# Two layers of attention and feed-forward in a planned kernel: when integer-route scores are sent, when GELU may begin, and GpSimd's effect in the planner's model

## The chip, the cores and the metric

The kernel runs on one core of one Trainium2 chip. The metric is the device time of one execution in microseconds (us). The kernel before took 1625.61 us, the median of three runs (1623.0 to 1626.69).

## What is computed

A sequence of 2048 tokens with 512 features passes through attention, feed-forward, attention and feed-forward again, each on a layer norm of its input and each added to the input. Both attentions share their weights, and so do both feed-forwards. There are 32 heads of 16 features, and the feed-forward is 1376 wide.

```python
def _A_ref(x, wqkv, wo):
    B, S, D = x.shape
    H = 32; Dh = D // H
    qkv = (lambda x, *d: x.transpose(*d))((x @ wqkv).reshape(B, S, 3, H, Dh), 2, 0, 3, 1, 4)
    q, k, v = qkv[0], qkv[1], qkv[2]
    scale = Dh ** -0.5
    scores = jnp.einsum("bhqd,bhkd->bhqk", q, k) * scale
    p = _softmax(scores, axis=-1)
    o = jnp.einsum("bhqk,bhkd->bhqd", p, v)
    return (lambda x, *d: x.transpose(*d))(o, 0, 2, 1, 3).reshape(B, S, D) @ wo
def _B_ref(x, w1, b1, w2, b2):
    y = _layernorm(x, axis=-1)
    h = _gelu(jnp.einsum("bsd,df->bsf", y, w1) + b1)
    return jnp.einsum("bsf,fd->bsd", h, w2) + b2
x = A_x
x = x + _A_ref(_layernorm(x, axis=-1), A_wqkv, A_wo)
x = x + _B_ref(_layernorm(x, axis=-1), B_w1, B_b1, B_w2, B_b2)
x = x + _A_ref(_layernorm(x, axis=-1), A_wqkv, A_wo)
x = x + _B_ref(_layernorm(x, axis=-1), B_w1, B_b1, B_w2, B_b2)
```

## The kernel before

**A planner writes the program.** Before anything is compiled, a small simulation in Python decides the order of the instructions on every engine. A job is a generator (`job_ffn`, `flow_scores` and others). It yields a `Task` for one engine, with a priority (smaller is more urgent) and a list of instructions, each with what it reads and writes and a duration in us; or it yields a condition: `keys` (events that must have been marked), `get` (a buffer from a pool), `ready` (the planner's clock has come near the time at which some data will be there). `Sched.run` (L437) picks again and again the task that could start earliest, by `best` (L380), where among those that are ready the priority decides. `Prog.op` (L105) then appends the instructions to their engine's stream and moves that engine's clock on by the modelled duration. So a modelled duration, a priority or a condition costs nothing on the chip by itself; it only decides the order. On the chip each engine runs its stream in that order, with semaphore waits between engines. A second pass, `refill` (L1176), puts matmuls on zeros (`zw`, L1281 to L1285) into gaps of TensorE (PE)[...].

**Scores.** `L` is 1 for the first pair of layers and 3 for the second. A *segment* (`build_segments`, L515) is one group of four heads (`hg`, 8 of them) with one unit of 512 queries (`qc`), against the keys of a part of the sequence. Mostly a segment has 64 *tiles*, each of 128 keys by 512 queries for one head. The first unit of each layer is cut in two parts by keys, of 16 and 48 tiles in the first layer and 48 and 16 in the second, and the last unit of the second layer is cut into two halves of 256 queries, whose segments have 32 tiles. That makes 88 segments with 4096 tiles. `flow_scores` (L1293) sends groups of three and two tiles in turn to PE (L1372, banks 0 to 4 of PSUM, four row tiles of 32 at once); each group goes through one exponential on ScalarE (ACT, L1357) into a buffer `PT`.

**The integer route.** Of every 16 blocks of 128 keys, five (`DK`) may be done without ScalarE. VectorE (DVE) takes the score tile from PSUM, adds a constant and writes 16-bit integers, whose bits read as bf16 are a coarse exponential (`d_load`, L1449). Three copies follow with the integer shifted by 32, 64 and 96 (`job_d`, L1480, two tiles at a time), and four PV matmuls with differently weighted values (`vs`) stand where one stood, so that the errors cancel. `take_d` (L1382) decides whether such a tile may be sent. It refuses when more than one score is on its way (`dload`), when VectorE's planned end is over 1.3 us ahead or over 2.0 us of its tasks are pending, when four batches are in work, when neither of its two PSUM banks (5, `DLANE`, and 7, `MISCB`, which projections and feed-forward use too) is near to being free, and, with fewer than 8 tiles left in the segment, when the next segment has already had four (two in the beginning). `take_d` is asked when a group is sent (`flow_scores`), when the planner sees a gap of over 0.5 us on PE (`fill_pe`), and by `d_solo` (L1429), which runs at the end of each load and first asks that VectorE's planned end and all its pending tasks add up to 1.2 us at most (`D_IDLE`).

**PV.** `try_pv` (L1497) sends the second matmuls (L1546, four column tiles at once, priority 1.0) into one accumulator, bank 6. At the end of a segment `job_segend` empties it by a transpose on VectorE (L1576); only then may the next segment's PV begin.

**Feed-forward.** When the eight segments of a unit are done, `job_post` runs the projection (L1632), residual (L1656) and norm (L832 to L845), and `job_ffn` (L1695) the first matmuls (L1687) with bias adds on VectorE (L1711), GELU on ScalarE as two instructions (L1717, ten blocks, and L1718, the last one), priority -1.0, which need another table than the exponential, the second matmuls (L1725), and residuals (L1727). In the first layer the norm and QKV of the second follow (`job_lnqkv`: L902, L908, L915, L925, scale L1088, queries L1118); in the second, the stores of the output (L1740). A unit's first matmuls wait until the unit before it is through. The priority of this work on PE is 2.2, and 0.95 for the last two units of the first layer. The last unit has its own end (`job_tail`).

**GpSimd (POOL)** makes the weighted values (L1143), the merges of the cut units (L1604 to L1607) and small things of the norms. `ln_apply` (L845), the query scaling (L1118) and the shifts (L1480) are VectorE instructions between tensors in SBUF. In the model of before, GpSimd does not affect them.

Of the kernel before, what the change touches and what calls it, by code (L numbers as in the profile page):

```python
# [14 lines left out]
ALU = mybir.AluOpType  # L15
# [48 lines left out]
class Prog:  # L64


    def __init__(self):
# [10 lines left out]
        self.drain = 0.0  # L78
        self.work = []
# [25 lines left out]
    def op(self, eng, fn, reads=(), writes=(), same_ok=(), dur=0.3, lat=None):  # L105
# [3 lines left out]
        q = None  # L109
        if eng == "sp":  # L110
            q = self.dma_rr
            self.dma_rr = (self.dma_rr + 1) % NDMAQ
            writes = writes + (("dmaq", q),)
        op = _Op(eng, fn, reads, writes)
# [23 lines left out]
        else:  # L138
            op.t1 = op.t0 + dur
# [131 lines left out]
class Sched:  # L271
# [4 lines left out]
    def __init__(self):  # L276
# [9 lines left out]
        self.filler = None  # L286

# [149 lines left out]
    def run(self):  # L437
        while True:
# [12 lines left out]
            t = pick[1]  # L451
# [8 lines left out]
            if t.cb is not None:  # L460
                t.cb()
        if self.live or self.kwait:
# [15 lines left out]
D_GAP = 0.5  # L478
DLANE = 5
D_IDLE = 1.2  # L480
D_PRIO = 0.5
# [16 lines left out]
class Builder:  # L498
# [344 lines left out]
    def ln_apply(self, tt, slot, i, dst, dres, prio):  # L843
        c = 4 * slot + i
        return Task("dve", prio, [I(lambda e: e.tensor_scalar(out=dst, in0=self.xres[:, tt, :], scalar1=self.mv[:, c, 0:1], scalar2=self.rs[:, c:c + 1], op0=ALU.subtract, op1=ALU.mult),  # L845
                                    [("x", tt), ("mv", c), ("rs", slot)], [dres], 0.407)])
# [263 lines left out]
    def job_qt(self, sg, s):  # L1110
# [8 lines left out]
                                  [RS, ("scl", k), ("qbias",)], [("qt", q)], 0.18 + 0.24 * W / 512)])  # L1119
# [8 lines left out]
    def job_vs(self, sg, i, kbs):  # L1128
# [9 lines left out]
        if L == 1:  # L1138
# [5 lines left out]
                                   [("V", hg, kb) for kb in kbs], [("vs", q, i + k2) for k2 in range(n)], 0.209 + 0.17 * n, [("vs", q, i + k2) for k2 in range(n)] if k > 1 else []) for k in (1, 2, 3)])  # L1144
# [148 lines left out]
    def flow_scores(self):  # L1293
# [11 lines left out]
        while True:  # L1305
# [14 lines left out]
            while len(grp) < G:  # L1320
# [4 lines left out]
                grp.append((sg, (sg["todo"] or sg["todod"]).pop(0)))  # L1325
            banks = list(range(b0, b0 + len(grp)))
# [102 lines left out]
    def d_solo(self):  # L1429

        S_ = self.S_
        if not self.wide or self.P.free["dve"] - S_.now + sum(o[4] for t in S_.pend["dve"] for o in t.ops) > D_IDLE:
            return
# [38 lines left out]
    def job_d(self, bt):  # L1472
# [4 lines left out]
        for k in range(1, len(SHIFT)):  # L1477
# [3 lines left out]
                                     [("dp", u, w) for w in range(n)], [("dp", v, w) for w in range(n)] + self.dres(v), 0.150 + 0.2605e-3 * N)])  # L1481
# [87 lines left out]
    def job_segend(self, sg):  # L1569
# [28 lines left out]
        if nparts == 2:  # L1598
# [5 lines left out]
            yield Task("pool", 1.2, [I(lambda e: e.tensor_tensor(out=M, in0=M, in1=dw.unsqueeze(2).broadcast_to([128, 16, 16]), op=ALU.mult), [RW, RO], [RO], 0.62),  # L1604
                                     I(lambda e: e.tensor_tensor(out=den, in0=den, in1=dw, op=ALU.mult), [RW, RD], [RD], 0.25),
                                     I(lambda e: e.tensor_tensor(out=T[:, :, 16], in0=T[:, :, 16], in1=den, op=ALU.add), [RD, RA], [RA], 0.26),
                                     I(lambda e: e.tensor_tensor(out=T[:, :, 0:16], in0=T[:, :, 0:16], in1=M, op=ALU.add), [RO, RA], [RA], 0.75)])  # L1607
# [87 lines left out]
    def job_ffn(self, L, qc):  # L1695
# [20 lines left out]
        HR = [("h", k) for k in range((NFC + 1) // 2)]  # L1716
        yield Task("act", -1.0, [I(lambda e: e.activation(out=self.gv[:, 0:nf * W], in_=hv[:, 0:nf * W], func=ACTF.Gelu_apprx_tanh), HR, HR, 1.5 + 0.427 * nf * W / 512, (), 1.313 + 0.2 + 0.427 * nf * W / 512),  # L1717
# [99 lines left out]
    def build(self):  # L1817
# [27 lines left out]
        S_.filler = self.fill_pe  # L1845
# [61 lines left out]
```

## Time and profile before

| | |
|---|---|
| median of three runs | 1625.61 us |
| the profiled execution | 1622.21 us, its span 1620.4 us |
| busy time: ACT, DVE, POOL | 1539.1 us, 1463.8 us, 195.9 us |
| exponentials (L1357) | 1288 for 3188 tiles, 1463.6 us |
| loads of the integer route (L1449) | 908, mean 680 ns |
| its shifts (L1480) | 1383, mean 422 ns |
| long GELUs (L1717) begin, after their table load | 332.8, 510.8, 694.9, 892.2, 1121.1, 1303.0, 1493.7 us; a short one 1587.4 us |
| a table load | 1283 ns |

Times in lines of the profile are us from the start of the span unless marked ns. PE is TensorE's matmuls, PEld its weight loads; L with a number is a line of the kernel's source. In a line of a group, the last part is the idle time of the engine just ahead of these instructions and what ended most of it; in a line of waits, the numbers are us in total, times and the longest. In a timeline, neighbouring records of one line are merged (x3), and brackets hold the idle time before the first.

### The profile page before, as it was taken

What the parts mean: (1) busy time and instruction counts of PE and PEld (TensorE: products, weight loads), DVE (VectorE), ACT (ScalarE), POOL (GpSimd) and SP (SyncE); (2) the same over time, 40 slices, a digit from 0 to 9 for tenths busy, and PEclk for the clock granted to TensorE, in tenths of its full rate; (3) what the DMA queues carried; (4) which work ended last, traced back from release to release, by engine and by line L of the source; (5) the groups of instructions that cost most, each with busy time, mean ns of one, the idle gap of its engine ahead of it and who ended that gap; (6) DMA issues with size and microseconds to landing.
All of it is one profiled execution on the core that took longest, in us unless ns stands there. A gap on an engine that the chain in (4) does not pass through costs nothing.

```text
span 1620.4 us, 39194 instructions
## 1 busy us (share of the span) xinstructions
PE 1582.4 (98%) x16531; PEld 481.8 (30%) x16531; DVE 1463.8 (90%) x3283; ACT 1539.1 (95%) x1369; POOL 195.9 (12%) x406
## 2 busy tenths in 40 slices
PE   9999999999999999999999999999999999999998
PEld 3222222222222222222222322222222222344454
DVE  7899999988998889979999799999899989999792
ACT  6998999999999999989999999999999999999993
POOL 4354210000100001001111124200000000000000
PEclk9999999999999999999999999999999999999999
DMA  6662011212311321224523232211102000121100
GB/s 173 118 159 66 21 30 25 60 30 69 90 47 33 65 70 44 63 60 107 104 44 63 62 92 40 56 29 24 27 16 46 21 25 15 40 47 33 39 22 21
DMA packets 212465, 88.80 MB, mean 55 GB/s; under 512 B 183835, under 2 KB 206656, under 8 KB 212288
## 3 DMA queue, kind: packets, MB, share of 16 engines
q1 hardware_dynamic: 212288, 86.29, 23.1%
q8 instruction: 129, 2.11, 0.6%
q14 instruction: 48, 0.39, 0.1%
HBM read 34.65 MB, written 19.48 MB: 33 GB/s over the span
## 4 chain that ended last, share of the span: by engine, by line
PE 43%; ACT 31%; DVE 22%; issue 2%; POOL 1%; DMA 0%; POOLq 0%; DVEq 0%
ACT PT L1357 29%; PE ps L1372 14%; PE ps L1546 12%; DVE dp L1449 8%; DVE dp L1480 6%; PE ps L1725 4%; PE ps L1687 4%; PE ps L902 3%; PE ps L1281 2%; ACT h L1717 2%; DVE accT L1576 1%; PE ps L1632 1%; DVE st L832 1%; DVE xn L1585 1%; PE ps L1283 1%
## 5 line engine op out<-in xcount | busy, mean ns | idle before, releaser
L1357 ACT ACTIVATE PT<-ps 128x1024 bf16<-128x1024 f32 (+1 forms) x1288 | 1463.6, 1273 | 44.9 <-PE ps L1372 39.9
L1372 PE MATMUL ps<-QT,KT 32*128 32x512 bf16 (+1 forms) x4608 | 680.6, 359 | 16.0 <-DVE dp L1449 7.6
L1449 DVE TENSOR_SCALAR dp<-ps 128x512 uint16<-128x512 f32 x908 | 608.5, 680 | 66.5 <-PE ps L1372 62.3
L1480 DVE TENSOR_SCALAR dp<-dp 128x1024 uint16<-128x1024 uint16 (+1 forms) x1383 | 525.0, 422 | 8.5 <-PE ps L1546 4.0
L1546 PE MATMUL ps<-PT,V 128*17 128x512 bf16 (+1 forms) x3583 | 469.4, 358 | 1.1 <-DVE accT L1576 1.1
L1546 PE MATMUL ps<-dp,vs 128*17 128x512 bf16 (+1 forms) x3075 | 435.5, 357 | 0.4 <-DVE dp L1480 0.2
L1372 PEld LDWEIGHTS ps<-QT,KT 32*128 32x128 bf16 x4608 | 169.0, 91 | 542.7 <-ACT PT L1357 271.6
L1283 PE MATMUL ps<-zw 32*128 32x444 bf16 (+2 forms) x814 | 223.8, 324 | 0.0
L1546 PE MATMUL ps<-dp,V 128*17 128x512 bf16 (+1 forms) x1025 | 205.1, 358 | 2.9 <-DVE accT L1576 2.7
L1285 PE MATMUL ps<-zw 128*32 128x448 bf16 (+17 forms) x1552 | 149.4, 324 | 0.6 <-DVE accT L1576 0.6
L1546 PEld LDWEIGHTS ps<-dp,vs 128*17 128x17 bf16 x3075 | 110.7, 88 | 127.8 <-issue 102.8
L1546 PEld LDWEIGHTS ps<-PT,V 128*17 128x17 bf16 x3583 | 111.1, 88 | 111.5 <-issue 99.1
L1281 PE MATMUL ps<-zw 128*128 128x448 bf16 (+22 forms) x573 | 137.1, 335 | 4.0 <-DVE ps L711 1.7
L840 POOL TENSOR_SCALAR rs<-mv 128x4 f32<-128x4 f32 (+2 forms) x19 | 4.3, 225 | 906.6 <-DVE mv L833 905.1
L1687 PE MATMUL ps<-yT,wf 128*128 128x512 bf16 (+3 forms) x396 | 103.0, 360 | 0.9 <-DVE yT L1808 0.5
L902 PE MATMUL ps<-wqkv,xnT 128*128 128x512 bf16 x336 | 92.8, 384 | 1.4 <-DVE qk L915 0.8
L1143 POOL TENSOR_SCALAR vs<-V 128x340 bf16<-128x340 bf16 (+2 forms) x72 | 61.1, 849 | 141.8 <-PE ps L1546 138.2
L1281 PEld LDWEIGHTS ps<-zw 128*128 128x128 bf16 x573 | 44.2, 98 | 88.8 <-issue 54.4
L1711 DVE TENSOR_SCALAR h<-ps,b1c 128x512 bf16<-128x512 f32 (+2 forms) x88 | 61.8, 702 | 7.1 <-PE ps L1687 6.9
L1546 PEld LDWEIGHTS ps<-dp,V 128*17 128x17 bf16 x1025 | 48.5, 88 | 53.4 <-issue 30.1
L1283 PEld LDWEIGHTS ps<-zw 32*128 32x128 bf16 x814 | 61.2, 92 | 1.6
L1576 DVE STREAM_TRANSPOSE accT<-ps 128x512 f32<-128x512 f32 (+1 forms) x88 | 57.9, 658 | 3.4 <-PE ps L1546 2.8
(171 smaller groups left out, 886.9 us busy)
## 6 DMA issues: line engine op xcount, KB each, us to landing
vs<-vs_scr SPq DMA_DIRECT2D x56, 255.0 KB, 2.6
wf<-in_B_w_dram SPq DMA_DIRECT2D x90, 128.0 KB, 2.6
q_scr<-qk SPq DMA_DIRECT2D x22, 256.0 KB, 2.1
k_scr<-qk SPq DMA_DIRECT2D x12, 256.0 KB, 2.0
out_dram<-xres SPq DMA_DIRECT2D x16, 128.0 KB, 1.7
vs_scr<-vs SPq DMA_DIRECT2D x8, 255.0 KB, 3.1
xres<-in_A_x_dram SPq DMA_DIRECT2D x7, 256.0 KB, 3.7
v_scr<-vst SPq DMA_DIRECT2D x12, 136.0 KB, 1.8
```

The lines of the kernel that those rows point to most:

```text
L902: yield Task("pe", prio, [I(lambda e, c=c: e.matmul(self.ps[:, b, :], lhsT=xnT[:, c, :], rhs=self.wqkv[:, c, which * 512:which * 512 + 512 ...
L1281: fn = lambda e: e.matmul(self.ps[:, b, 0:w], lhsT=self.zw[:, 0:128], rhs=self.zw[:, 0:w], start=st, stop=st, skip_group_check=True)
L1283: fn = lambda e: e.matmul(self.ps[:, b, 0:w], lhsT=self.zw[32 * p:32 * p + 32, 0:128], rhs=self.zw[32 * p:32 * p + 32, 0:w], start=st, sto ...
L1285: fn = lambda e: e.matmul(self.ps[32 * p:32 * p + 32, b, 0:w], lhsT=self.zw[:, 0:32], rhs=self.zw[:, 0:w], start=st, stop=st, skip_group_c ...
L1357: S_.submit(Task("act", 1e-5 * gi, [I(lambda e, pt=pt, n=n, b0=b0: e.activation(out=self.PT[:, pt:pt + n, :], in_=self.ps[:, b0:b0 + n, :] ...
L1372: return [I(lambda e, kb=kb, i=i: e.matmul(self.ps[:, b, i * W:(i + 1) * W], lhsT=self.KT[32 * hp:32 * hp + 32, hg, kb * 128:(kb + 1) * 12 ...
L1449: self.S_.submit(Task("dve", 0.0, [I(lambda e: e.tensor_scalar(out=self.dp[:, u, w * 512:(w + 1) * 512], in0=self.ps[:, b, :], scalar1=BIT ...
L1480: yield Task("dve", pr, [I(lambda e, k=k, v=v: e.tensor_scalar(out=self.dp[:, v, 0:N], in0=self.dp[:, u, 0:N], scalar1=float(SHIFT[k]), sc ...
L1546: ops.append((nth[j, sh] + 0.1 * i, I(lambda e, hp=hp, v=v, ap=ap[:, i * W:(i + 1) * W], first=first and i == 0, W=W: e.matmul(self.ps[32 ...
L1576: yield Task("dve", 0.3, [I(lambda e: e.transpose(self.accT[:, a, 0:W], self.ps[:, ACCB, 0:W]), [("ps", ACCB)], [RA], 0.17 + 0.535 * W / 5 ...
L1687: yield Task("pe", pr, [I(lambda e, c=c: e.matmul(self.ps[0:M, b, off:off + W], lhsT=self.w1(fc, c), rhs=self.yT[:, c, 0:W], start=(c == 0 ...
L1725: yield Task("pe", pr, [I(lambda e, fc=fc, i=i, b=b: e.matmul(self.ps[:, b, :], lhsT=self.gt(fc, i, W), rhs=self.w2(L, fc), start=(fc == 0 ...
```

## The change

It has three parts, all in the planner; no instruction is added to or taken from the program but for what follows from how many tiles take which route.

First, `d_solo` is asked after every VectorE task that has been planned (`after_dve`), besides at the end of each load, and it counts as pending only those tasks that can start within 0.5 us (`D_NEAR`). The conditions in `take_d` stay.

Second, before GELU is handed to ScalarE, `job_ffn` waits until its input is nearly there, and then for a mark of the scores: of the current segment 30% of the tiles must have been taken, and where more than 50% have been already, it is the next segment whose 30% is waited for. In the last segment there is no such wait.

Third, the model knows of GpSimd: `Prog.op` keeps the last GpSimd instruction's start, end and effect (`hit`), and a VectorE instruction marked "fast" that overlaps it is planned longer by 0.09 (L1143), 0.28 (L1604) or 0.38 us (L1607). Two base durations are set a little lower.

```diff
--- before.py
+++ after.py
@@ -76,6 +76,7 @@
         self.tiling = "full"
         self.tiles = {}
         self.drain = 0.0
+        self.hit = (0.0, 0.0, 0.0)
         self.work = []
 
     def ready(self, eng, reads, writes, same_ok=()):
@@ -136,6 +137,13 @@
             self.work.append((op.t0, op.t1, 1.0 if how == "full" else 0.25))
             self.free[eng] = op.t0 + min(dur, PE_ISSUE)
         else:
+            if eng == "pool":
+                self.hit = (op.t0, op.t0 + dur, lat or 0.0)
+                lat = None
+            elif lat == "fast":
+                if self.hit[0] < op.t0 + dur and op.t0 < self.hit[1]:
+                    dur += self.hit[2]
+                lat = None
             op.t1 = op.t0 + dur
             self.free[eng] = op.t0 + (max(0.02, dur - OVERLAP[eng]) if lat is None else lat)
         deps = {}
@@ -284,6 +292,7 @@
         self.live = 0
         self.timers = []
         self.filler = None
+        self.after_dve = None
 
     def submit(self, task, cb=None):
         self.seq += 1
@@ -459,6 +468,8 @@
                 self.P.op(t.eng, fn, reads, writes, same_ok, dur, lat)
             if t.cb is not None:
                 t.cb()
+            if t.eng == "dve" and self.after_dve is not None:
+                self.after_dve()
         if self.live or self.kwait:
             raise RuntimeError("scheduler stuck: %d live, keys %s, pools %s" % (self.live, list(self.kwait)[:8], [(n, len(p.free), len(p.waiters)) for n, p in self.pools.items() if p.waiters]))
 
@@ -476,8 +487,11 @@
 FILL_SLACK = 0.02
 READ_SLACK = 0.4
 D_GAP = 0.5
+GELU_FROM = 0.3
+GELU_TO = 0.5
 DLANE = 5
 D_IDLE = 1.2
+D_NEAR = 0.5
 D_PRIO = 0.5
 DBATCH = 2
 DFLY = 4
@@ -843,7 +857,7 @@
     def ln_apply(self, tt, slot, i, dst, dres, prio):
         c = 4 * slot + i
         return Task("dve", prio, [I(lambda e: e.tensor_scalar(out=dst, in0=self.xres[:, tt, :], scalar1=self.mv[:, c, 0:1], scalar2=self.rs[:, c:c + 1], op0=ALU.subtract, op1=ALU.mult),
-                                    [("x", tt), ("mv", c), ("rs", slot)], [dres], 0.407)])
+                                    [("x", tt), ("mv", c), ("rs", slot)], [dres], 0.395, (), "fast")])
 
     def dma(self, fn, reads, writes, prio, dur=0.08, lat=None):
         return Task("sp", prio, [I(fn, reads, writes, dur, (), lat)])
@@ -1116,7 +1130,7 @@
         W = sg["W"]
         src, RS = (self.psbf(self.q0bank)[:, 0:512], ("ps", self.q0bank)) if s is None else (self.qraw[:, s, 0:W], ("qraw", s))
         yield Task("dve", 0.4, [I(lambda e: e.tensor_scalar(out=self.QT[:, q, 0:W], in0=src, scalar1=self.scl[:, k, hg:hg + 1], scalar2=self.qbias[:, 0:1], op0=ALU.mult, op1=ALU.add),
-                                  [RS, ("scl", k), ("qbias",)], [("qt", q)], 0.18 + 0.24 * W / 512)])
+                                  [RS, ("scl", k), ("qbias",)], [("qt", q)], 0.16 + 0.24 * W / 512, (), "fast")])
         if s is None:
             self.S_.release("mb", self.q0bank)
         else:
@@ -1141,7 +1155,7 @@
         yield ("keys", self.kv_keys(sg, kbs))
         src = self.V[:, hg, kbs[0]:kbs[-1] + 1:3, :, :].rearrange("p k h d -> p k (h d)")
         yield Task("pool", 0.8, [I(lambda e, k=k: e.tensor_scalar(out=self.vs[:, q, k - 1, i:i + n, :], in0=src, scalar1=WSHIFT[k], scalar2=None, op0=ALU.mult),
-                                   [("V", hg, kb) for kb in kbs], [("vs", q, i + k2) for k2 in range(n)], 0.209 + 0.17 * n, [("vs", q, i + k2) for k2 in range(n)] if k > 1 else []) for k in (1, 2, 3)])
+                                   [("V", hg, kb) for kb in kbs], [("vs", q, i + k2) for k2 in range(n)], 0.209 + 0.17 * n, [("vs", q, i + k2) for k2 in range(n)] if k > 1 else [], 0.09) for k in (1, 2, 3)])
         for kb in kbs:
             self.S_.mark(("vs", sg["i"], kb))
         d = DK.index(kbs[0])
@@ -1323,6 +1337,9 @@
                     break
                 sg = self.segs[self.cur]
                 grp.append((sg, (sg["todo"] or sg["todod"]).pop(0)))
+            for sg, j in grp:
+                if sg["nt"] - self.left(sg) >= GELU_FROM * sg["nt"]:
+                    S_.mark(("under", sg["i"]))
             banks = list(range(b0, b0 + len(grp)))
             keys = [("ret", b) for b in banks] + [("free", last[b]) for b in banks if b in last]
             for sg, j in grp:
@@ -1429,7 +1446,7 @@
     def d_solo(self):
 
         S_ = self.S_
-        if not self.wide or self.P.free["dve"] - S_.now + sum(o[4] for t in S_.pend["dve"] for o in t.ops) > D_IDLE:
+        if not self.wide or self.P.free["dve"] - S_.now + sum(o[4] for t in S_.pend["dve"] if S_.task_ready(t) <= S_.now + D_NEAR for o in t.ops) > D_IDLE:
             return
         d = self.take_d([])
         if d is not None:
@@ -1478,7 +1495,7 @@
             v = yield ("get", "dp", sg["i"])
             pr = 0.15 if not self.left(sg) and sg is self.segs[self.acc_seg] else 0.5 if self.left(sg) < DURGE else 2.5
             yield Task("dve", pr, [I(lambda e, k=k, v=v: e.tensor_scalar(out=self.dp[:, v, 0:N], in0=self.dp[:, u, 0:N], scalar1=float(SHIFT[k]), scalar2=None, op0=ALU.add),
-                                     [("dp", u, w) for w in range(n)], [("dp", v, w) for w in range(n)] + self.dres(v), 0.150 + 0.2605e-3 * N)])
+                                     [("dp", u, w) for w in range(n)], [("dp", v, w) for w in range(n)] + self.dres(v), 0.150 + 0.2605e-3 * N, (), "fast")])
             self.d_ready(bt, k, v, range(n))
         self.flying -= 1
         self.use_done(("dp", u))
@@ -1601,10 +1618,10 @@
             yield Task("dve", 1.2, [I(lambda e: e.tensor_tensor(out=dw, in0=rowT[:, :, 16], in1=self.rowA[:, hg, :], op=ALU.subtract), [RX, ("rowA", hg)], [RW], 0.17)])
             S_.release("xn", xs)
             yield Task("act", -1.0, [I(lambda e: e.activation(out=dw, in_=dw, func=ACTF.Exp, scale=EXPS), [RW], [RW], 0.23)])
-            yield Task("pool", 1.2, [I(lambda e: e.tensor_tensor(out=M, in0=M, in1=dw.unsqueeze(2).broadcast_to([128, 16, 16]), op=ALU.mult), [RW, RO], [RO], 0.62),
+            yield Task("pool", 1.2, [I(lambda e: e.tensor_tensor(out=M, in0=M, in1=dw.unsqueeze(2).broadcast_to([128, 16, 16]), op=ALU.mult), [RW, RO], [RO], 0.62, (), 0.28),
                                      I(lambda e: e.tensor_tensor(out=den, in0=den, in1=dw, op=ALU.mult), [RW, RD], [RD], 0.25),
                                      I(lambda e: e.tensor_tensor(out=T[:, :, 16], in0=T[:, :, 16], in1=den, op=ALU.add), [RD, RA], [RA], 0.26),
-                                     I(lambda e: e.tensor_tensor(out=T[:, :, 0:16], in0=T[:, :, 0:16], in1=M, op=ALU.add), [RO, RA], [RA], 0.75)])
+                                     I(lambda e: e.tensor_tensor(out=T[:, :, 0:16], in0=T[:, :, 0:16], in1=M, op=ALU.add), [RO, RA], [RA], 0.75, (), 0.38)])
         rv = self.rv[:, a, 0:nb]
         yield Task("dve", 1.2, [I(lambda e: e.reciprocal(out=rv, in_=T[:, :, 16]), [RA], [("rv", a)], 0.245)])
         if L == 3 and qc == len(self.units[3]) - 1 and hg == 7:
@@ -1714,6 +1731,11 @@
         S_.mark(("ffn1", L, qc))
         yield ("keys", [("h", L, qc, fc) for fc in range(NFC)])
         HR = [("h", k) for k in range((NFC + 1) // 2)]
+        yield ("ready", "act", HR)
+        if self.cur + 1 < len(self.segs):
+            sg = self.segs[self.cur]
+            late = sg["nt"] - self.left(sg) > GELU_TO * sg["nt"]
+            yield ("keys", [("under", self.cur + 1 if late else self.cur)])
         yield Task("act", -1.0, [I(lambda e: e.activation(out=self.gv[:, 0:nf * W], in_=hv[:, 0:nf * W], func=ACTF.Gelu_apprx_tanh), HR, HR, 1.5 + 0.427 * nf * W / 512, (), 1.313 + 0.2 + 0.427 * nf * W / 512),
                                 I(lambda e: e.activation(out=self.g10[0:self.FLAST, 0:W], in_=hv[0:self.FLAST, nf * W:(nf + 1) * W], func=ACTF.Gelu_apprx_tanh), HR, [("g10",)], 0.2 + 0.427 * W / 512, (), 0.2 + 1.32 + 0.427 * W / 512)])
         GR = HR + [("g10",)]
@@ -1843,6 +1865,7 @@
         S_.when([("retq", 4), ("retq", 5)], lambda: [S_.release("dp", u) for u in range(8, 12)])
         S_.when([("qt", 0)], lambda: S_.spawn(self.flow_scores(), 0.0))
         S_.filler = self.fill_pe
+        S_.after_dve = self.d_solo
         self.P.spare = lambda: (tuple(range(6)) if self.wide and ("scores_done",) not in S_.done else ()) + ((MISCB,) if MISCB in S_.pools["mb"].free else ())
         for L in (1, 3):
             for qc in range(len(self.units[L])):
```

## The prediction

> **What bounds the kernel now.** I read the page's busy shares, the groups, the waits, then tables by stretch and timelines of the places they pointed to.
>
> ```profile
> PE 1582.4 (98%) x16531; PEld 481.8 (30%) x16531; DVE 1463.8 (90%) x3283; ACT 1539.1 (95%) x1369; POOL 195.9 (12%) x406
> ```
> ```profile
> L1357 ACT ACTIVATE PT<-ps 128x1024 bf16<-128x1024 f32 (+1 forms) x1288 | 1463.6, 1273 | 44.9 <-PE ps L1372 39.9
> ...
> L1449 DVE TENSOR_SCALAR dp<-ps 128x512 uint16<-128x512 f32 x908 | 608.5, 680 | 66.5 <-PE ps L1372 62.3
> L1480 DVE TENSOR_SCALAR dp<-dp 128x1024 uint16<-128x1024 uint16 (+1 forms) x1383 | 525.0, 422 | 8.5 <-PE ps L1546 4.0
> ...
> L1281 PE MATMUL ps<-zw 128*128 128x448 bf16 (+22 forms) x573 | 137.1, 335 | 4.0 <-DVE ps L711 1.7
> ```
> PE's 98% holds filler (L1281, L1283 and L1285 multiply zeros). The real limit is exponentials, made on two routes. There are 4096 score tiles; 908 go to VectorE (L1449), so 3188 go to ScalarE, at 1463.6 / 3188 = **0.459 us of ScalarE a tile**. On VectorE a tile costs (608.5 + 525.0) / 908 = **1.248 us**. From 88 to 1572 us, while both routes are open, the table by stretch has ScalarE 1444.34 and VectorE 1374.52 of 1484 us: ScalarE misses 40 us, VectorE 109. So ScalarE is the bound, and each tile that VectorE can still take shortens its work by 0.459 us.
>
> ```profile
> DVE dp L1449 <- PE ps L1372: 62.3, 97, 2.3
> DVE xres L1727 <- PE ps L1725: 27.5, 16, 4.2
> ...
> ACT PT L1357 <- PE ps L1372: 39.9, 76, 3.3
> ```
> Most of VectorE's idle time is a wait for a score tile that was sent late. The timeline of VectorE shows how:
> ```profile
> 361.62 0.68 DVE L1449 TENSOR_SCALAR dp<-ps 128x512 uint16<-128x512 f32 x1
> 363.27 0.69 DVE L1449 TENSOR_SCALAR dp<-ps 128x512 uint16<-128x512 f32 x1 [0.97 <-PE ps L1372]
> 363.99 1.10 DVE L1480 TENSOR_SCALAR dp<-dp 128x1024 uint16<-128x1024 uint16 x3
> 365.21 0.69 DVE L1449 TENSOR_SCALAR dp<-ps 128x512 uint16<-128x512 f32 x1
> ```
> After the first tile of a pair nothing is queued, and the next score is sent only when that load has ended: 0.97 us idle here, 0.4 to 1.0 us in each pair that follows.
>
> The second loss lies at the feed-forward activations (GELU). This table gives 20 us from the start of six of the seven long ones (columns: stretch, length, busy PE, PEld, DVE, ACT, POOL):
> ```profile
> 331.50:351.50 20.00, 19.66 (x192) 5.51 (x188) 18.35 (x42) 19.59 (x16) 0.00 (x0) 1.00 0.03 6
> 509.50:529.50 20.00, 19.64 (x178) 5.66 (x177) 17.77 (x39) 19.78 (x15) 0.00 (x0) 1.00 0.01 2
> 693.60:713.60 20.00, 18.99 (x154) 6.36 (x152) 11.67 (x26) 19.51 (x15) 0.00 (x0) 1.00 0.09 25
> 890.90:910.90 20.00, 18.79 (x153) 6.43 (x150) 13.07 (x28) 19.52 (x15) 3.26 (x5) 1.00 0.06 16
> ...
> 1301.70:1321.70 20.00, 19.39 (x173) 5.54 (x166) 16.23 (x37) 19.66 (x15) 0.00 (x0) 1.00 0.09 24
> 1492.30:1512.30 20.00, 18.99 (x297) 8.31 (x289) 13.64 (x32) 19.45 (x16) 0.00 (x0) 1.00 0.19 48
> ```
> The same table for L1449 alone counts 15, 15, 6, 8, 12 and 9 loads. Counting tiles in the order of the trace (L1357's by width, L1449's as one) places the GELUs in their segments at tiles 19/64, 37/64, 2/64, 3/48, 2/64 and 18/32 (the seventh, at 1119.8, at 8/64). Those just past a boundary starve VectorE:
> ```profile
> 702.70 0.69 DVE L1727 TENSOR_TENSOR xres<-ps,xres 128x512 bf16<-128x512 f32 x1 [3.96 <-PE ps L1725]
> 703.35 0.72 DVE L1576 STREAM_TRANSPOSE accT<-ps 128x512 f32<-128x512 f32 x1
> ```
> The old segment's last tiles sit behind the GELU on ScalarE, so its accumulator (bank 6) is emptied only at 703.35; while its tiles are still to be taken, the new segment may send four tiles by VectorE, and their PV waits. ScalarE pays later: at 713.4 and 910.7 it waits 3.32 us each.
>
> **What the Trainium skill says.** "Perfetto Trace Analysis", section "Identifying the Most-Contended Engine", holds occupancy to be fair for Vector and Scalar and poor for matmuls; the filler agrees. "ScalarE: Activation LUTs", "What ACT_TABLE_LOAD costs", gives 1283 ns and some 1380 ns of drain for each switch; the trace has 1.28 us and gaps of 0.02 us, no such drain. "TensorEngine Tiling (Array Packing)", "Key Properties", says that a change of tiling mode drains the engine: a score sent alone buys such a change. "SBUF — State Buffer", "SBUF: two separate sides", has the pair that VectorE and GpSimd share locked for a whole instruction; here L1480 takes 416 ns alone and 509 beside L1143 (849 ns): a part of it.
>
> **The change, part by part.**
>
> *Integer-route scores.* It asks after every planned VectorE task, and counts only work ready within 0.5 us. While a load runs, the next score can then go to the second bank (7), where today it waits for the load's end. To gain are the 62.3 us of L1449's waits. Not all: bank 7 also serves projections, a tile may be sent at most two at a time, near a segment's end four tiles bound it, and PE needs its round trip. I take half, 32 us: 32 / 1.248 = 26 tiles, 26 x 0.459 = **-11.8 us**. Ends: 0 (banks bind) and all, 50 tiles, -23. Each tile adds three PV matmuls of a quarter array (3 x 0.216 / 4 = 0.16 us; ten of L1725 start in 2.16 us) and a lone score (0.22): 26 x 0.38 = 10 us of PE, hidden in the filler's place (L1281's 137.1 us); without that cover up to +10. On VectorE a load (0.68) goes ahead of transposes, bias adds and residual adds.
>
> *GELU.* Nothing is added or taken away on ScalarE (1.28 + 4.47 + 0.63 + 1.28 = 7.7 us each); it begins later. Wanted is the picture of the windows at 331.5 and 509.5, where VectorE works 18.1 of 20 us. The other four lack 6.4, 5.0, 1.8 and 4.4, together 17.6 us. I take 60%, 10.6 us: 8.5 tiles, **-3.9 us**; and the two waits of 3.32 us on ScalarE, **-6.6 us**. Ends: 0 and -13.1. The wait is one of the planner: no engine's queue stands still for it, since the planner puts other exponentials ahead. But all that follows a GELU goes later with it: 44 matmuls (L1725), four residual adds, and in the first layer the norms, QKV matmuls and their transposing and storing DMAs on SP and the pow on GpSimd; in the second the output DMAs, 0.33 us of SP's issue each. SP has room between its issues there.
>
> Where is there slack? The first three GELUs: their keys are loaded from 763 us on for the segment that starts at 818. The fourth (890.9): by the timeline its chain ends in the scale (L1088) at 969 and the query (L1118) at 970, and by the count of tiles the segment needing them starts at 973.7: 3 us of slack against a move from 3/48 to 30% of 48, 12 tiles x 0.36 us = 4.3: **+1.5 us**. The seventh (1492.4, at 56%, later with the tiles picked ahead) falls past the half and goes to the next segment: 14 + 6 tiles x 0.36 = 7.2 us later, and its followers have no slack:
> ```profile
> 1543.94 42.12 ACT L1357 ACTIVATE PT<-ps 128x1024 bf16<-128x1024 f32 x37
> 1586.08 1.28 ACT L1717 ACT_TABLE_LOAD   x1
> ...
> 1584.86 0.48 DVE L1711 TENSOR_SCALAR h<-ps,b1c 96x256 bf16<-96x256 f32 x1 [1.19 <-PE ps L1687]
> ```
> The last GELU's input is ready at 1585.3, ScalarE is done with scores at 1586.1; the tail hangs on both. A delay of 7.2 us is partly made up, since PE and banks come free when scores end: I take **+5**, between +2 and +7.2.
>
> *GpSimd in the model.* L1480 overlapping L1143, L1604 or L1607 is stretched by 93, 178 and 414 ns on 46, 13 and 12 records: 11.6 us that the plan did not know and now knows. The stretch stays; only order changes: 0, between -2 and +2.
>
> *Sum.* -11.8 - 3.9 - 6.6 + 1.5 + 5 = **-15.8 us**. The profiled execution took 1622.2 us (span 1620.4 and 1.8 around it): 1606.4. The median shown, 1625.6, lies 3.4 above it: **1609.8 us**, forecast 1610.
>
> **Rivals.**
> *Supply binds, not the trigger:* banks and the limit of four refuse the extra scores; then part one gives 2 us and the GELU's half stays: -2 - 10.5 + 6.5 = -6, 1619.6. For it: gaps of L1449 near boundaries, which no trigger helps. Against: the regular gap inside pairs.
> *The postponed GELU hits chains without slack (slower):* place, the fourth GELU before 973.7 and the seventh to last before 1586; price 4.3 + 7.2 = 11.5 us if nothing is made up, more if busier VectorE and PE slow the bias adds (L1711) and L1687. It decides once the rest gains less than that; with 4 us of gain it is +7.5, 1633. For it: the 0.8 us between 1585.3 and 1586.1. Against: PE drains quickly once scores stop.
> *It does little:* the plan's order shifts, gains and losses cancel: 1625.
>
> **Chances.** Forecast 0.54 (own range 1598 to 1619), supply 0.18, chains 0.17, little 0.11. A measurement tells about 0.2% from no change, 3.3 us: faster is below 1622.4, slower above 1628.9. Faster: all of the forecast, 0.15 of supply and 0.03 of little, 0.72; same: 0.03 + 0.08 = 0.11; slower 0.17. The range runs from near the full yield of the first part (both parts in full, costs as taken: -23.0 - 13.1 + 6.5 = -29.6, 1596) to inside the slower case, 1630.
>
> **What would show it.** Right: L1449 near 940 instead of 908, its wait for PE near 30 us; L1357's time down by some 15 us; at 0.3 to 0.5 of a segment every long GELU, with some 15 loads in its 20 us; no ScalarE wait of 3.3 us. Wrong: L1449's count unmoved; ScalarE idle before 974; a gap between the last exponential and the last L1717. The forecast fails if tiles rise but ScalarE's idle time rises as much.

## The result and the profile after

The changed kernel takes **1601.89 us** (median of four runs, 1601.2 to 1603.4), the kernel before 1624.3 us beside it (median of four, 1621.76 to 1626.69). The ratio is 0.9864 with a 95% interval of 0.9845 to 0.9882: 22.4 us faster, where 15.8 had been forecast. The span of the profiled execution went from 1620.4 to 1601.8 us, 18.6 us less. A part of the 22.4 us goes with the clock that TensorE was granted: 30 further runs of the kernel before show 0.993 to 0.999 of full speed and take longer the lower it is (median 1621.2 us for the ten at 0.999, 1628.9 for the three at 0.993), while the changed kernel's four runs show 1.0, so that at nearly the same clock it is 19.3 us faster.

The page of the changed kernel, busy shares and then the groups that answer to those shown of before (L1374 was L1357, L1466 was L1449, L1497 was L1480; of the lines below, L1389 was L1372, L1739 was L1717, L1704 was L1687):
```profile
PE 1571.1 (98%) x16532; PEld 481.3 (30%) x16532; DVE 1473.8 (92%) x3323; ACT 1535.5 (96%) x1366; POOL 207.0 (13%) x406
...
L1374 ACT ACTIVATE PT<-ps 128x1024 bf16<-128x1024 f32 (+1 forms) x1283 | 1457.1, 1269 | 36.0 <-PE ps L1389 30.1
...
L1466 DVE TENSOR_SCALAR dp<-ps 128x512 uint16<-128x512 f32 x921 | 618.7, 683 | 56.7 <-PE ps L1389 54.0
L1497 DVE TENSOR_SCALAR dp<-dp 128x1024 uint16<-128x1024 uint16 (+1 forms) x1410 | 533.0, 421 | 7.4 <-PE ps L1563 3.3
```
The integer route has 921 tiles instead of 908, and the exponentials take 6.5 us less. That is about a third of the 18.6 us. VectorE still waits 54.0 us for scores (62.3 before).

The waits of ScalarE in the changed kernel (us in total, times, longest):
```profile
ACT PT L1374 <- PE ps L1389: 30.1, 66, 6.0
ACT h L1801 <- PE ps L1704: 14.2, 4, 10.4
```
Before, these were 39.9 and 21.4. The second is a wait in the end after the last score: the end became shorter. The longest of the first is new: 6.0 us at one place, the first segment of the second part of the second layer (segment 48, counted from 0).

The table of 20 us from the start of the seven long GELUs in the changed kernel, the fifth left out (columns: stretch, length, busy PE, PEld, DVE, ACT, POOL, then the granted clock and the DMA's share and GB/s):
```profile
330.60:350.60 20.00, 19.57 (x181) 5.68 (x174) 18.10 (x40) 19.91 (x16) 0.00 (x0) 1.00 0.01 2
517.30:537.30 20.00, 19.98 (x199) 5.55 (x196) 17.67 (x41) 19.91 (x16) 0.00 (x0) 1.00 0.03 8
687.70:707.70 20.00, 19.70 (x168) 5.50 (x167) 17.23 (x40) 19.92 (x15) 0.00 (x0) 1.00 0.02 5
881.20:901.20 20.00, 19.74 (x167) 5.76 (x167) 14.90 (x34) 18.47 (x13) 2.80 (x5) 1.00 0.08 16
...
1293.80:1313.80 20.00, 19.84 (x207) 6.13 (x201) 17.21 (x40) 19.81 (x16) 0.00 (x0) 1.00 0.04 11
1473.50:1493.50 20.00, 19.25 (x312) 8.82 (x304) 12.38 (x30) 19.69 (x15) 0.00 (x0) 1.00 0.18 45
```
VectorE's column shows the third GELU mended (17.23 us busy instead of 11.67), the fourth mended by little (14.90 instead of 13.07), the seventh not (12.38 instead of 13.64). Over all seven VectorE works 115.68 us instead of 108.84. By the count of tiles they now stand at 33/64, 18/64, 20/64, 16/48, 18/64, 18/64 and 7/32.

The end in the timeline of ScalarE, changed kernel:
```profile
1567.25 1.28 ACT L1739 ACT_TABLE_LOAD   x1
1568.55 2.34 ACT L1739 ACTIVATE h<-h 128x2560 bf16<-128x2560 bf16 x1
1570.92 0.42 ACT L1740 ACTIVATE g<-h 96x256 bf16<-96x256 bf16 x1
1571.35 1.28 ACT L1374 ACT_TABLE_LOAD   x1
1572.64 3.28 ACT L1374 ACTIVATE PT<-ps 128x1024 bf16<-128x1024 f32 x3
1576.15 1.02 ACT L1374 ACTIVATE PT<-ps 128x1024 bf16<-128x1024 f32 x1 [0.22 <-PE ps L1389]
```
The last GELU, which came behind the last exponential, now comes ahead of the last four groups. From the last exponential on, the kernel needs 24.6 us instead of 34.4.

**Where the 18.6 us are.** I cut both spans at the same tiles (where the last tile of segments 7, 34, 44, 48, 79 and 86 starts, counted from 0, by counting L1357's and L1449's tiles in order), and took ScalarE's idle time in each piece:

| segments | before, us | after, us | difference | of it ScalarE idle |
|---|---|---|---|---|
| start to 7 | 88.5 | 89.2 | +0.7 | +0.4 |
| 8 to 34 | 603.6 | 590.0 | -13.6 | -9.9 |
| 35 to 44 (GELUs 3 and 4) | 225.7 | 221.1 | -4.6 | -4.8 |
| 45 to 48 | 62.0 | 67.4 | +5.4 | +6.2 |
| 49 to 79 | 505.5 | 502.0 | -3.5 | -0.2 |
| 80 to 86 | 87.0 | 89.2 | +2.2 | +0.2 |
| 87 and the end | 48.2 | 42.8 | -5.4 | |

The largest piece, segments 8 to 34, has neither of the starving GELUs in it. No step of the prediction had put so much there. Two places hold most of its idle time. In segments 8 to 10 ScalarE idles 5.4 us before and 2.8 after; here TensorE worked at half the clock for 6.8 us in the profiled execution of before (the clock stands behind POOL's column), and nowhere in this piece in that of the changed kernel:
```profile
125.60:132.40 6.80, 6.80 (x37) 1.00 (x34) 4.52 (x13) 4.18 (x4) 1.00 (x4) 0.50 0.10 39
```
In segments 31 to 34 it idles 6.4 us before and 1.2 after, and most of that is three waits for scores:
```profile
607.83 45.77 ACT L1357 ACTIVATE PT<-ps 128x1024 bf16<-128x1024 f32 x40 [2.80 <-PE ps L1372]
655.18 22.70 ACT L1357 ACTIVATE PT<-ps 128x1024 bf16<-128x1024 f32 x20 [1.59 <-PE ps L1372]
679.13 11.63 ACT L1357 ACTIVATE PT<-ps 128x1024 bf16<-128x1024 f32 x10 [1.25 <-PE ps L1372]
```
In the whole of segments 8 to 34 the changed kernel has no wait over 0.62 us. That asked for experiments.

### The profile page after: what moved, and what is told of

Same layout as the page of the kernel before. It is cut to its first block, busy times and chain, and to the rows that moved or that the text cites. A ratio compares the mean times of both kernels' runs of the same rounds, so it can differ in the third digit from the quotient of the medians.

```text
span 1601.8 us, 39236 instructions
## 1 busy us (share of the span) xinstructions
PE 1571.1 (98%) x16532; PEld 481.3 (30%) x16532; DVE 1473.8 (92%) x3323; ACT 1535.5 (96%) x1366; POOL 207.0 (13%) x406
## 4 chain that ended last, share of the span: by engine, by line
PE 49%; ACT 28%; DVE 20%; issue 1%; DMA 1%; POOL 1%; POOLq 0%; DVEq 0%
ACT PT L1374 25%; PE ps L1389 17%; PE ps L1563 14%; DVE dp L1466 7%; DVE dp L1497 5%; PE ps L1747 4%; PE ps L1704 4%; PE ps L916 4%; PE ps L1295 3%; ACT h L1739 2%; PE ps L1299 1%; DVE accT L1593 1%; PE ps L1297 1%; DVE st L846 1%; PE ps L1649 1%
## 5 line engine op out<-in xcount | busy, mean ns | idle before, releaser
L1374 ACT ACTIVATE PT<-ps 128x1024 bf16<-128x1024 f32 (+1 forms) x1283 | 1457.1, 1269 | 36.0 <-PE ps L1389 30.1
L1389 PE MATMUL ps<-QT,KT 32*128 32x512 bf16 (+1 forms) x4608 | 672.5, 358 | 11.5 <-DVE dp L1466 2.2
L1466 DVE TENSOR_SCALAR dp<-ps 128x512 uint16<-128x512 f32 x921 | 618.7, 683 | 56.7 <-PE ps L1389 54.0
L1497 DVE TENSOR_SCALAR dp<-dp 128x1024 uint16<-128x1024 uint16 (+1 forms) x1410 | 533.0, 421 | 7.4 <-PE ps L1563 3.3
L1563 PE MATMUL ps<-dp,vs 128*17 128x512 bf16 (+1 forms) x3120 | 441.0, 357 | 0.7 <-DVE dp L1497 0.6
L1389 PEld LDWEIGHTS ps<-QT,KT 32*128 32x128 bf16 x4608 | 169.9, 91 | 541.8 <-ACT PT L1374 260.4
L1563 PE MATMUL ps<-dp,V 128*17 128x512 bf16 (+1 forms) x1040 | 214.5, 357 | 2.3 <-DVE accT L1593 2.0
L1297 PE MATMUL ps<-zw 32*128 32x444 bf16 (+2 forms) x714 | 197.6, 325 | 0.0
L1299 PE MATMUL ps<-zw 128*32 128x448 bf16 (+23 forms) x1621 | 142.6, 318 | 0.7 <-DVE dp L1466 0.6
L1295 PE MATMUL ps<-zw 128*128 128x448 bf16 (+17 forms) x560 | 130.6, 334 | 4.1 <-DVE dp L1466 2.2
L1704 PE MATMUL ps<-yT,wf 128*128 128x512 bf16 (+3 forms) x396 | 103.5, 360 | 1.0 <-DVE yT L1830 0.5
L1728 DVE TENSOR_SCALAR h<-ps,b1c 128x512 bf16<-128x512 f32 (+2 forms) x88 | 62.3, 708 | 1.8 <-PE ps L1704 1.5
L1299 PEld LDWEIGHTS ps<-zw 128*32 128x32 bf16 x1621 | 52.4, 95 | 24.7 <-DVE dp L1466 5.7
```

Source lines behind the costliest of these rows:

```text
L1295: fn = lambda e: e.matmul(self.ps[:, b, 0:w], lhsT=self.zw[:, 0:128], rhs=self.zw[:, 0:w], start=st, stop=st, skip_group_check=True)
L1297: fn = lambda e: e.matmul(self.ps[:, b, 0:w], lhsT=self.zw[32 * p:32 * p + 32, 0:128], rhs=self.zw[32 * p:32 * p + 32, 0:w], start=st, sto ...
L1299: fn = lambda e: e.matmul(self.ps[32 * p:32 * p + 32, b, 0:w], lhsT=self.zw[:, 0:32], rhs=self.zw[:, 0:w], start=st, stop=st, skip_group_c ...
L1374: S_.submit(Task("act", 1e-5 * gi, [I(lambda e, pt=pt, n=n, b0=b0: e.activation(out=self.PT[:, pt:pt + n, :], in_=self.ps[:, b0:b0 + n, :] ...
L1389: return [I(lambda e, kb=kb, i=i: e.matmul(self.ps[:, b, i * W:(i + 1) * W], lhsT=self.KT[32 * hp:32 * hp + 32, hg, kb * 128:(kb + 1) * 12 ...
L1466: self.S_.submit(Task("dve", 0.0, [I(lambda e: e.tensor_scalar(out=self.dp[:, u, w * 512:(w + 1) * 512], in0=self.ps[:, b, :], scalar1=BIT ...
```

## The experiments

Three theories stood against each other. **A**: the three parts add up, each by its own mechanism. **B**: a large part hangs on the place of the last GELU ahead of the last exponentials. **C**, formed after the first seven runs: the plan of before is an unlucky one, and almost any other order is better.

### Each part alone

e1_solo_only, of the diff only these edits and the lines that set them up (the marks in `flow_scores` and `hit` stand in it too, and in e2_gelu_only and e7_no_model, but nothing uses them there):
```diff
+            if t.eng == "dve" and self.after_dve is not None:
+                self.after_dve()
...
-        if not self.wide or self.P.free["dve"] - S_.now + sum(o[4] for t in S_.pend["dve"] for o in t.ops) > D_IDLE:
+        if not self.wide or self.P.free["dve"] - S_.now + sum(o[4] for t in S_.pend["dve"] if S_.task_ready(t) <= S_.now + D_NEAR for o in t.ops) > D_IDLE:
...
+        S_.after_dve = self.d_solo
```


> The kernel before with the first part alone (d_solo asked after every VectorE task, and only work ready within 0.5 us counted). The plan has 921 loads of the integer route instead of 908, so 13 tiles leave ScalarE, 6 us of its work. Theory A (the parts add up, each by the cost in the prediction): 8 to 12 us under the kernel before. Theory B (a large part of the gain of the whole is the last GELU's place ahead of the last exponentials, which needs the feed-forward chain to be early): 4 to 7 us under, unless the chain happens to be early here too, which its timeline would show.

Measured: 1610.2 us, ratio 0.9912 (0.9895 to 0.9929), 14.6 us under the kernel before (1624.8 us beside it), more than either theory gave. Its last GELU begins at 1574.9, 5.1 us ahead of the end of the last exponential, and the end, from there on, takes 28.4 us: theory B had left this case open.

e2_gelu_only, of the diff only the marks in `flow_scores` and, in `job_ffn`:
```diff
+        yield ("ready", "act", HR)
+        if self.cur + 1 < len(self.segs):
+            sg = self.segs[self.cur]
+            late = sg["nt"] - self.left(sg) > GELU_TO * sg["nt"]
+            yield ("keys", [("under", self.cur + 1 if late else self.cur)])
```


> The kernel before with the second part alone (GELU from 30% of a segment). 906 loads. Theory A: the two waits of 3.3 us on ScalarE and the idle VectorE behind GELUs 3, 4 and 6 go: 7 to 10 us under the kernel before. Theory B: the same inside the layers, but the seventh GELU goes later, and the last one stays behind the last exponential: 2 to 6 us under.

Measured: 1606.19 us, ratio 0.9891 (0.9876 to 0.9906), 18.6 us under, about twice what theory A gave and three times theory B's most. The last GELU comes 13.3 us ahead and the end takes 21.1 us.

e3_model_only, of the diff, among what is used, only `hit` in `Prog.op`, the added `0.09`, `0.28`, `0.38` and `"fast"`, and the two durations:
```diff
+            if eng == "pool":
+                self.hit = (op.t0, op.t0 + dur, lat or 0.0)
+                lat = None
+            elif lat == "fast":
+                if self.hit[0] < op.t0 + dur and op.t0 < self.hit[1]:
+                    dur += self.hit[2]
+                lat = None
```


> The kernel before with the third part alone (GpSimd's effect in the model). 905 loads. Both theories: within 3 us of the kernel before; only the order changes. More than 4 us either way would mean that a mere change of order is worth as much as the other parts.

Measured: **1600.78 us**, ratio 0.9855 (0.984 to 0.9869). The part that was to bring nothing brings 24.0 us, all of the gain, with 905 tiles on the integer route, fewer than before. The timeline of its ScalarE at the end:
```profile
1556.73 1.28 ACT L1734 ACT_TABLE_LOAD   x1
1558.02 2.34 ACT L1734 ACTIVATE h<-h 128x2560 bf16<-128x2560 bf16 x1
...
1562.12 15.29 ACT L1374 ACTIVATE PT<-ps 128x1536 bf16<-128x1536 f32 x13
1577.42 1.28 ACT L1776 ACT_TABLE_LOAD   x1
```
The last GELU is 19 us ahead, and from 1577.4 to the end of the span at 1598.2 are 20.8 us. In segments 8 to 34 ScalarE idles 8.1 us instead of 18.2. Theory A falls here: the three together would give 57 us, and give 22.

### All but one part

e5_no_solo, e6_no_gelu and e7_no_model are the changed kernel without the edits of e1_solo_only, e2_gelu_only and e3_model_only, for example for e6_no_gelu:
```diff
-        yield ("ready", "act", HR)
-        if self.cur + 1 < len(self.segs):
-            sg = self.segs[self.cur]
-            late = sg["nt"] - self.left(sg) > GELU_TO * sg["nt"]
-            yield ("keys", [("under", self.cur + 1 if late else self.cur)])
```


> The changed kernel without its first part: GELU's window and the model stay. 907 loads. Theory A: 8 to 12 us slower than the changed kernel, 1610 to 1614. Theory B: as much if the feed-forward chain falls late again and the last GELU lands behind the exponentials (5 us) on top of 14 tiles more on ScalarE (6 us); only 6 us if the last GELU stays ahead of them.

> The changed kernel without its second part. 913 loads. Theory A: 7 to 10 us slower than the changed kernel, 1609 to 1612, with the waits of over 3 us on ScalarE behind the third and fourth GELU back. Theory B: as much or more only where the last GELU also goes behind the last exponential.

> The changed kernel without its third part. 920 loads. Both theories: within 3 us of the changed kernel, 1599 to 1605. If it is over 5 us slower, knowing GpSimd's effect is worth something, or order alone moves the time by that much; the timeline of the end (is the last GELU ahead of the last exponential?) and of the segment that starts the second part of the second layer would tell which.

Measured: 1607.28 us without the first part (ratio to before 0.9909, 0.9878 to 0.9939), 1608.12 without the second (0.9905, 0.9887 to 0.9924), 1601.64 without the third (0.9865, 0.9846 to 0.9883). The first two are 5.4 and 6.2 us slower than the changed kernel, each somewhat less than theory A gave. Theory B's 6 us fits e5_no_solo, whose last GELU stays ahead; for e6_no_gelu, where it stays ahead too, B had named no figure. The third is as expected. But the model alone is the best of the three alone, and with one of the other parts added it becomes 6 to 7 us worse. Parts that interact like this are not three mechanisms with a price each.

### Changes that mean nothing

e8_before_exp_1ns and e9_before_transpose_5ns are the kernel before, e10_after_exp_1ns is the changed kernel, each with one number of the model moved:
```diff
-... 0.19 + 0.4275 * n)]),
+... 0.191 + 0.4275 * n)]),
```
(e8_before_exp_1ns and e10_after_exp_1ns)
```diff
-... 0.17 + 0.535 * W / 512)])
+... 0.17 + 0.54 * W / 512)])
```
(e9_before_transpose_5ns)

> The kernel before with one number of the model changed that means nothing: an exponential's planned duration is 1 ns longer. 905 loads. Theory C (the plan of before is an unlucky one, with the last GELU behind the last exponential and a slow stretch between 500 and 700 us, and most of the gain is that any other order avoids these): 10 to 20 us under the kernel before. Theory A (the parts themselves bring the gain): within 3 us of the kernel before.

> The kernel before with another number of the model changed that means nothing: the transpose that empties the accumulator is planned 5 ns longer. 914 loads. Theory C: 10 to 20 us under the kernel before. Theory A: within 3 us of it, but for 3 us from six more tiles on VectorE.

> The changed kernel with the planned duration of an exponential 1 ns longer. 922 loads. Theory A: within 3 us of the changed kernel, 1599 to 1605, because its parts hold whatever the order. Theory C: the changed kernel's own place is chance too; it lands within the spread of the other plans, 1600 to 1611.

Measured: 1615.03 us (ratio to before 0.9943, 0.9924 to 0.9963), 1608.8 us (0.9909, 0.9881 to 0.9937) and 1602.39 us (0.9868, 0.9851 to 0.9884). One nanosecond in a planned duration moves the kernel before by 8.3 us, five nanoseconds in another by 14.5. Against the ten runs of before at a clock of 0.999 (1621.2 us), e8_before_exp_1ns, whose runs show 0.999 and 1.0, is 6.2 us faster, and the two of e9_before_transpose_5ns at 0.999 (1604.65 and 1605.98) are 15.9 us faster, so the clock alone does not make them differ. The first lies just under the 10 to 20 us that theory C gave, the second inside; theory A, which had 3 us for both (6 with the six tiles), is out, at the same clock too. For e10_after_exp_1ns theory A and C both fit.

### The place of the last GELU

e4_last_gelu_end, the changed kernel with
```diff
+        if L == 3 and qc == len(self.units[3]) - 2:
+            yield ("keys", [("scores_done",)])
         yield ("ready", "act", HR)
```


> The changed kernel, but the GELU of the unit before the last (the eighth, the short one) must wait until the last scores have been sent. Theory B: it goes behind the last exponential as in the kernel before, the end from the last exponential on grows from 24.6 us to about 34 us while the scores end about 4.5 us earlier: 5 us slower than the changed kernel, some 1607. Theory A (the end is bound by the last unit's attention, not by this GELU): within 1.5 us of the changed kernel, 1602.

Measured: 1606.16 us (ratio to before 0.9889, 0.9875 to 0.9904), 4.3 us slower than the changed kernel's 1601.89, which was timed in another session; the spans of the two profiled executions, 1604.5 and 1601.8, differ by 2.7. The timeline of its ScalarE:
```profile
1554.48 15.50 ACT L1374 ACTIVATE PT<-ps 128x1024 bf16<-128x1024 f32 x14
1570.00 1.28 ACT L1741 ACT_TABLE_LOAD   x1
```
The GELU stands behind the last exponential, and from 1570.0 to the end of the span at 1604.5 are 34.6 us, as in the kernel before. Theory B had 5 us for it: this GELU's place is worth 3 to 4 us here.

e11_before_end_first, the kernel before with
```diff
-        return 0.95 if L == 1 and qc >= self.NC - 2 else 2.2
+        return 0.95 if L == 1 and qc >= self.NC - 2 or L == 3 and qc == self.NC - 1 else 2.2
```


> The kernel before, but the feed-forward of the unit before the last has priority 0.95 on PE instead of 2.2, so that its GELU comes ahead of the last exponentials; all of the plan up to 1485 us stays as it was. 909 loads. If the place of the last GELU is worth what e4_last_gelu_end showed in the other direction, together with what the end gains by an early chain: 8 to 13 us under the kernel before, with the same times up to 1485 us. If the end is bound elsewhere: within 3 us of it.

Measured: 1614.11 us, ratio 0.9947 (0.9926 to 0.9967), 9.2 us under the kernel before, with the segments up to the seventh GELU as they were there (from segment 14 on each ends 1.9 to 2.1 us earlier, most of it from segment 10 and from before it). Around segment 10 the order is the same, but TensorE is at half the clock for 3.4 us instead of 6.8, and in that segment ScalarE idles 0.9 us instead of 2.2:
```profile
124.00:127.40 3.40, 3.27 (x16) 0.69 (x16) 2.10 (x8) 1.05 (x2) 1.02 (x4) 0.50 0.21 80
```
So of the 9.1 us between the two spans about 7 belong to the GELU's place; the four runs at a clock of 0.999 have a median of 1613.6 us, 7.6 less than the ten of before. The timeline of its ScalarE:
```profile
1567.50 1.28 ACT L1717 ACT_TABLE_LOAD   x1
...
1585.69 4.20 ACT L1357 ACTIVATE PT<-ps 128x1536 bf16<-128x1536 f32 x4 [0.18 <-PE ps L1372]
1589.91 1.28 ACT L1759 ACT_TABLE_LOAD   x1
```
The exponentials end at 1589.9, 3.8 us later than before since a GELU and two table loads now lie among them, and 21.4 us later all is done, instead of 34.4.

Over all runs, the end follows the lead. Lead is the time from the start of the last L1717 (or its like, behind its table load) to the end of the last exponential; the end is what follows that exponential:

| run | lead, us | end, us |
|---|---|---|
| before | -1.3 | 34.4 |
| e4_last_gelu_end | -1.3 | 34.6 |
| e1_solo_only | 5.1 | 28.4 |
| e8_before_exp_1ns | 7.8 | 25.8 |
| after | 8.6 | 24.6 |
| e10_after_exp_1ns | 11.6 | 22.5 |
| e2_gelu_only | 13.3 | 21.1 |
| e7_no_model, e9_before_transpose_5ns | 17.1, 17.5 | 21.3, 21.8 |
| e3_model_only, e11_before_end_first | 19.4, 21.1 | 20.8, 21.4 |
| e6_no_gelu, e5_no_solo | 22.4, 25.2 | 23.1, 21.1 |

With less lead than about 12 us, each us of it shortens the end by about one. With more, the end is 21 to 23 us; that this is the last unit's own chain was not tested.

e12_after_end_first, the same edit in the changed kernel:

> The changed kernel with the edit of e11_before_end_first: the feed-forward of the unit before the last has priority 0.95 on PE. In the runs so far the stretch from the last exponential to the end is 34 us with the last GELU behind the exponentials and 21 to 22 us with its start 12 us or more ahead of their end; in the changed kernel it starts 8.7 us ahead and the stretch is 24.6 us. So 3 us faster than the changed kernel, some 1599, if the scores before it are not slowed; if they are slowed by PE work that now goes ahead of PV, as in e11_before_end_first (scores 3.8 us later), within 2 us of the changed kernel.

Measured: 1599.14 us (1597.33 to 1601.22), ratio to before 0.985 (0.9818 to 0.9881). The interval covers the changed kernel's 0.9864, so the times don't tell the two apart. In the trace the segments agree to within a microsecond up to segment 72, the lead is 27 us, the end 21.2 us instead of 24.6, and the exponentials end 1.0 us later: 2.4 us of span. That is the best median of all the kernels here; the gain of 3 us over the changed kernel that had been expected is not shown by the times.

## Why the prediction was right, and where its steps were not

The total was near: -15.8 forecast, -22.4 measured, with faster as the likely side and 1602 inside the range. The sum under it was not, so that the total came near is luck: the terms of the first two parts were too large, another had the wrong sign, and a part of the 22.4 us is the lower clock of before, which was in no term. Of the signs that were to show it right, none came in full (921 loads and not some 940; 54.0 us of waits and not 30; the exponentials down by 6.5 us and not 15; 8 to 13 loads behind four of the seven GELUs; a wait of 6.0 us on ScalarE), and one of the signs of being wrong came: ScalarE idle before 974.

**"Integer-route scores", -11.8.** The mechanism is seen, at half its size: 13 tiles instead of 26, 6.0 us. VectorE's wait for scores fell to 54.0 us, not to 30. Counting in the plan who sends each tile tells where the rest went: `d_solo` sends 447 instead of 291 (through bank 7, as forecast, 80 instead of 19), but groups of `flow_scores` take only 400 instead of 502 along and PE's gaps 74 instead of 115. The new trigger for the most part sends what another would have sent: 156 more by it, 143 fewer by the others. The term should have been net of the other senders. What a score sent alone costs by the change of tiling mode, which the prediction names, no run isolates.

**"GELU", -3.9 and -6.6.** VectorE gained 6.8 us in the seven windows (115.68 - 108.84), where 10.6 had been taken for four of them. The two waits of 3.32 us went; waits of 1.2 to 2.6 us stand in their region. Segments 35 to 44 are 4.6 us shorter in all. The mechanism is seen, at about half its price. Whether it is worth anything in the time the runs leave open: e3_model_only has no such part, and its third and sixth GELU begin at tiles 4/64 of their segments, and it is as fast as the changed kernel.

**"The fourth GELU", +1.5.** ScalarE's timeline in the changed kernel has
```profile
952.79 4.79 ACT L1374 ACTIVATE PT<-ps 128x1536 bf16<-128x1536 f32 x4
963.60 12.75 ACT L1374 ACTIVATE PT<-ps 128x1536 bf16<-128x1536 f32 x11 [6.03 <-PE ps L1389]
```
The prediction's second rival, chains without slack, is seen here in its place, at 6 us: the chain to the scale and the query had no slack. The cause is not that the GELU was held (it begins at 881, right after its last bias add), but that the scores came to segment 48 17.1 us sooner (the last tile before it starts at 956.6 instead of 973.7) and the scale (L1102, L1088 before) only 7.3 us sooner (962.0 instead of 969.3). I had priced a delay, and not that the other side would be early.

**"The seventh GELU", +5.** This step failed, with its sign. The GELU was held, by 8 us after its bias adds (1465 to 1473.5), but it still came earlier against the scores, 3.8 us behind the start of segment 79's last tile instead of 7.1: the first matmuls before it had taken 35 us and not 41. The last GELU then came ahead of the last exponentials, and the last piece lost 5.4 us; that the one followed from the other was not tested. I had seen that tail and exponentials both ended at 1586, and read it as a chain without slack; I had not asked what the kernel would gain if the chain came earlier. e4_last_gelu_end and e11_before_end_first show that it gains, in both directions.

**"GpSimd in the model", between -2 and +2.** Wrong by the most: e3_model_only gives -24.0. But e8_before_exp_1ns and e9_before_transpose_5ns give -8.3 and -14.5 (-6 and -16 at the same clock) for edits that say nothing of GpSimd, so nothing shows that knowing the effect is what helps. I had bounded a change of order by the size of the durations changed. The time follows the order without such a bound: a wait at segment 48 is 6 us long, and a GELU on the wrong side of the last exponentials cost 3 to 4 us in one kernel and about 7 in the other.

**What the gain is made of.** For the kernel before theory C fits best: each of the other plans is faster, by 8 to 24 us, though two of them hold nothing but a changed number. In segments 8 to 34 ScalarE idles 18.2 us there and 7 to 15 us in every other plan (but for e11_before_end_first, which shares this stretch with it), and it alone of the unforced plans has the last GELU behind the exponentials. Plans with neither of the first two parts take 1624, 1615, 1609 and 1601 us (without e11_before_end_first); with one of them 1610, 1606, 1607 and 1608; with both 1602, 1602 and 1602. The three with both agree to within 1 us, which speaks for those parts as a guard against bad plans; with four and three plans this is argued and not shown. Of the 10 us of idle time that segments 8 to 34 lost, 2.6 lie in segments 8 to 10, around the stretch at half the clock, and 5.2 in segments 31 to 34, with the three waits of 1.25 to 2.80 us. What in the order makes these waits stays open, and so does whether the order brings the lower clock about; these runs don't isolate it.

## What to carry to other kernels

Where a planner or a list of priorities decides the order, measure first how much the time moves under a change that means nothing; here 1 ns in a model moved it by 8 us (6 at the same clock), and a gain of that size is no evidence for the edit that came with it. Look at the end by itself: the work of the unit before the last should be through before the bound engine is done, and a more urgent priority for it was worth about 7 us in the kernel before. Compare runs at the same granted clock, where the runs of one kernel differ in it. When a stage is sped up, ask of each chain that runs beside it whether it is now late.

## What was not expected of the hardware

Nothing in these runs contradicted the durations read from the first trace: a table load took 1.28 us in all of them, with the next instruction 0.01 us behind it (but for one load near the start, behind which ScalarE waits for TensorE's first results). What the prediction left out is the clock: in the profiled executions of eight of the fourteen kernels TensorE is granted half the clock for 3.4 to 10.2 us in all, ahead of the end, and in the 30 runs of the kernel before the time rises from 1621 to 1629 us as the mean clock falls from 0.999 to 0.993. All other surprises were of order.
